# Releasing and casting batch 1's v on ScalarE, and cutting the key-value products of batches 4 to 7 into thirds

## The chip, the cores and the metric

The kernel runs on one core of one Trainium2 chip. The core has TensorE (PE: products, and loads of the stationary operand, PEld), VectorE (DVE), ScalarE (ACT), GpSimd (POOL) and SyncE (SP, which only issues transfers here). Each engine works through its own list of instructions in order; semaphores tie the lists together. The metric is the time of one execution on the device in microseconds. Before the change the median of three runs is 283.88 us (283.86 to 284.46).

## The reference

Eight batches of eight heads, 576 rows of 64 numbers each. Softmax of q goes over the 64 numbers of a row, softmax of k over the 576 rows; the small matrix kv of each head is multiplied onto q. Then comes a two-layer block over all 4,608 rows.

```python
q_s = softmax(q, axis=-1)               # (8, 8, 576, 64)
k_s = softmax(k, axis=2)
kv = np.einsum('bhsd,bhse->bhde', k_s, v)
x = np.einsum('bhsd,bhde->bhse', q_s, kv)
x = x.transpose(0, 2, 1, 3).reshape(8 * 576, 512)
h = x @ w_in                            # (4608, 2048)
out = np.maximum(0.01 * h, h) @ w_out   # (4608, 512)
```

## The kernel before

The two-layer block is cut into nine tiles of 512 rows. Layer 1 (L506) of a tile is 64 products of 512 columns into PSUM tiles `ph`; ScalarE applies the leaky function (L515) and leaves `gj`. Layer 2 (L527) is 64 products of 512 columns into `pout`; a copy (L521) and two stores follow for each 128 rows. Tile 0 differs: its layer 1 is done in two halves of 256 columns, in which `end_act` applies the function to pairs of columns groups j, j+1, and its layer 2 takes the four row groups in turn for each j. So each j of layer 2 needs one more column of `w_out_sb`, which arrives in eight pieces of two columns, issued by GpSimd.

The attention of batch b stands in between. Its inputs come by SP's queue (`load`). A core's partition holds 9 rows (R) of a head, and two halves of four heads each; H0 and H1 are slices of these. For k: the maximum over rows (`k_tree`, `k_allmax`), subtraction (`k_sub`), exponential (`k_exp`, ScalarE). For v: a cast to bf16 into `vb` (`v_cast`, once for each pair of heads gg = 0 and 1, so gg = 0 reads H0 and gg = 1 reads H1). The key-value products (`kv_quads`, L311) are 36 for each gg: for each of the 9 rows four products of 64x64 weights and 65 columns, one on each quarter of PE's array. The 65th column is a column of ones and gives the denominator. `kd_make` divides by it. The attention products (`cross`, L430) take `kd` as weights and the transposed q as columns; `attend` allocates two PSUM tiles and makes the four products of one or two gg. `x_keep` copies the result into `xT`, the input of layer 1.

The order of the work is written out by hand. `at(t, u, ...)` hangs functions on point u of tile t; for tile 0 the points 0 to 31 come after the leaky functions of the two halves (point 16 + j is column group j of the second half) and the points 32 to 47 after each j of layer 2. From tile 1 on, points 0 to 15 follow the column groups of layer 1 and points 16 to 31 follow every fourth product of layer 2. What a function emits goes to the end of each engine's list at that moment.

Three places matter.

- `more_loads` (L630), at point 20 of tile 0: it takes a buffer for batch 1's v, has GpSimd write one element of it from `kmax` (L632), and then issues v's two halves on SP. Because the transfers overwrite that element, they wait for the write, and the write waits for the maximum of batch 1's k. Behind them in SP's queue stands `hold_sync(1, ...)`, a small transfer that waits for w_out columns 10 and 11, and then the loads of batch 2.
- Points 20 and 32 of tile 0: GpSimd casts v's gg = 1 at the end of its list for batch 1, behind two subtractions for q and one for k; ScalarE casts gg = 0 and then does the exponential of k's half H0. At point 43 `kv(1)` makes 36 products of gg = 0, then 36 of gg = 1.
- `attend_kv(b)` (L457), at one point of each of the tiles 2 to 5, for b = 3 to 6: the long attention products of batch b (rows 0 to 7 of R: two fours of 512 columns), eight short ones for the last row, then the 72 key-value products of batch b+1. The short products and the key-value sums share two PSUM tiles `pokv`. PSUM tiles of one tag rotate through six buffers.

Of the kernel before, what the change touches and what calls it, by code (L numbers as in the profile page):

```python
# [20 lines left out]
R = 9  # L21
# [4 lines left out]
def kernel(  # L26
# [9 lines left out]
    nc = tc.nc  # L36
# [3 lines left out]
    B, H, S, D = q.shape  # L40
# [31 lines left out]
    def raw(name):  # L72
        return raw_pool.tile([P, HL, R, D], FP32, name=name, tag="raw")
# [13 lines left out]
    ALLH, ALLR = slice(0, HL), slice(0, R)  # L87
    RA, RB = slice(0, 4), slice(4, R)
    R1, R2, R3 = slice(4, 6), slice(6, 8), slice(8, R)
    st = [{} for _ in range(B)]  # L90
# [11 lines left out]
    identf = const_pool.tile([P, P], FP32)  # L102
# [29 lines left out]
    def k_begin(b):  # L132
        st[b]["ke"] = ke_pool.tile([P, R, HL, D], BF16, name="ke")
        st[b]["kmax"] = mx_pool.tile([P, HL, D], FP32, name="kmax")
        st[b]["kmaxT"] = mx_pool.tile([P, HL * D], FP32, name="kmaxT")
        st[b]["kall"] = mx_pool.tile([P, HL, D], FP32, name="kall")

    def k_tree(b, hs, steps=slice(0, 4)):
        n = hs.stop - hs.start
        ks = st[b]["k"][:, hs]  # L140
        if steps.start == 0:
            st[b]["t4"] = mx_pool.tile([P, HL, 4, D], FP32, name="t4")[:, 0:n]
        t4 = st[b]["t4"]
        t2, t1 = t4[:, :, 0:2], t4[:, :, 0]
        for o, i0, i1 in (
            (t4, ks[:, :, 0:4], ks[:, :, 4:8]),
            (t2, t2, t4[:, :, 2:4]),
            (t1, t1, t4[:, :, 1]),
            (st[b]["kmax"][:, hs], t1, ks[:, :, 8]),
        )[steps]:  # L150
            nc.vector.tensor_tensor(out=o, in0=i0, in1=i1, op=ALU.max)  # L151
# [29 lines left out]
    def k_sub(eng, b, hs):  # L181
        ks = st[b]["k"][:, hs]
        n = hs.stop - hs.start
        eng.tensor_tensor(  # L184
            out=ks,
            in0=ks,
            in1=st[b]["kall"][:, hs].unsqueeze(2).to_broadcast([P, n, R, D]),
            op=ALU.subtract,
        )

    def k_exp(b, hs):
        nc.scalar.activation(  # L192
            out=st[b]["ke"][:, :, hs].rearrange("p r h d -> p h r d"),
            in_=st[b]["k"][:, hs],
            func=AF.Exp,
        )

    def v_cast(eng, b, gg):
        o = vb2[b % 2][:, :, gg, :, 0:D].rearrange("p r h d -> p h r d")
        i = st[b]["v"][:, 2 * gg : 2 * gg + 2]  # L200
        if eng is nc.scalar:
            eng.copy(out=o, in_=i)
        else:
            eng.tensor_copy(out=o, in_=i)  # L204


    def q_begin(b):
        st[b]["qe"] = qe_pool.tile([P, R, HL, D], BF16, name="qe")
        if b < 2:
            st[b]["qT"] = qT_pool.tile([P, NB, R, L], BF16, name="qT", tag="qT")  # L210
# [70 lines left out]
    def q_exp(b, rs, hs=ALLH):  # L281
        nc.scalar.activation(  # L282
            out=st[b]["qe"][:, rs, hs].rearrange("p r h d -> p h r d"),
            in_=st[b]["q"][:, hs, rs],
            func=AF.Exp,
        )
# [16 lines left out]
        )  # L303


    def kv_quads(b, gg, outs):
        for r in range(R):
            for hp in range(2):
                for hh in range(2):
                    rows = slice(hh * L, (hh + 1) * L)  # L310
                    nc.tensor.matmul(  # L311
                        outs[hh][hp * D : (hp + 1) * D, 0 : D + 1],
                        lhsT=st[b]["ke"][rows, r, 2 * gg + hp],
                        rhs=vb2[b % 2][rows, r, gg, hp, 0 : D + 1],
                        start=(r == 0),
                        stop=(r == R - 1),
                    )

    def kv(b):

        pkv = [psB_pool.tile([P, 2, D + 2], FP32, name="pkv", tag=BANK_TAG) for _ in range(2)]
        for gg in range(2):
            kv_quads(b, gg, [pkv[hh][:, gg] for hh in range(2)])
        st[b]["pkv"] = pkv

    def kd_make(b):
        for hh in range(2):
            pkv = st[b]["pkv"][hh]
            krec = small_pool.tile([P, 2, 1], FP32, name="krec")
            nc.vector.reciprocal(out=krec, in_=pkv[:, :, D : D + 1])  # L330
            nc.vector.tensor_tensor(
                out=kd2[b % 2][:, :, hh],
                in0=pkv[:, :, 0:D],
                in1=krec.to_broadcast([P, 2, D]),
                op=ALU.mult,
            )
# [101 lines left out]
    def attend(b, ggs, rows):  # L438
        n = (rows.stop - rows.start) * L
        ps = [  # L440
            psB_pool.tile([P, len(ggs), n], FP32, name="po", tag=BANK_TAG) for _ in range(2)
        ]
        for i, gg in enumerate(ggs):
            cross(b, gg, [ps[hp][:, i] for hp in range(2)], rows)
        st[b]["po", ggs, rows.start] = ps

    def x_keep(eng, b, ggs, rows, hp):
        ps = st[b]["po", ggs, rows.start][hp]
        c0, c1 = b * S + rows.start * L, b * S + rows.stop * L
        s0 = 2 * ggs[0] + hp  # L450
        o = xT[:, s0 : 2 * ggs[-1] + hp + 1 : 2, c0:c1]
        if eng is nc.scalar:
            eng.copy(out=o, in_=ps)  # L453
        else:
            eng.tensor_copy(out=o, in_=ps)

    def attend_kv(b, rows=slice(0, 8), rest=slice(8, R)):  # L457
        keep = attend_rows(b, rows)
        n = 2 * (rest.stop - rest.start) * L
        both = [psB_pool.tile([P, n + 2 * (D + 2)], FP32, name="pokv", tag=BANK_TAG) for _ in range(2)]  # L460
        ps = [a[:, 0:n].rearrange("p (g c) -> p g c", g=2) for a in both]
        st[b + 1]["pkv"] = pkv = [a[:, n:].rearrange("p (g d) -> p g d", g=2) for a in both]
        for gg in range(2):
            cross(b, gg, [ps[hp][:, gg] for hp in range(2)], rest)
        for gg in range(2):
            kv_quads(b + 1, gg, [pkv[hh][:, gg] for hh in range(2)])
        st[b]["po", (0, 1), rest.start] = ps
        kd_make(b + 1)
        for fn in keep:
            fn()  # L470
        for hp in range(2):
            x_keep(nc.scalar, b, (0, 1), rest, hp)

    def attend_rows(b, rows, engs=(nc.scalar, nc.scalar)):
        groups = ((0, 1),) if rows.stop - rows.start <= 4 else ((0,), (1,))
        for ggs in groups:
            attend(b, ggs, rows)
        return [
            lambda ggs=ggs, hp=hp: x_keep(engs[hp], b, ggs, rows, hp) for ggs in groups for hp in range(2)
        ]  # L480
# [57 lines left out]
    def at(t, u, *fns):  # L538
        while t > 0 and u >= 32:
            t, u = t + 1, u - 32  # L540
        hooks.setdefault((t, u), []).extend(fns)
# [5 lines left out]
    H0, H1 = slice(0, 2), slice(2, 4)  # L547
# [9 lines left out]
    def hold_sync(i, src):  # L557
        nc.sync.dma_start(out=held[:, i], in_=src)
# [70 lines left out]

    def more_loads():  # L630
        st[1]["v"] = t = raw("v_raw")
        nc.gpsimd.tensor_copy(out=t[0:1, 0, 0, 0:1], in_=st[1]["kmax"][0:1, 1, D - 1 : D])  # L632
        load(v, 1, "v_raw", [(H0, ALLR), (H1, ALLR)], t)
        hold_sync(1, w_out_sb[0:1, 11, 0:128])
        st[2]["k"] = load(k, 2, "k_raw", [(H0, ALLR)])
        load(q, 1, "q_raw", [(ALLH, RE)], st[1]["q"])
        load(k, 2, "k_raw", [(H1, ALLR)], st[2]["k"])
        st[2]["q"] = load(q, 2, "q_raw", [(ALLH, ALLR)])
        st[2]["v"] = load(v, 2, "v_raw", [(ALLH, ALLR)])


    at(0, 19, lambda: q_max(0, R3), lambda: q_sub(nc.vector, 0, R3), lambda: q_exp(0, R3))
    at(0, 20, lambda: k_begin(1), lambda: q_begin(1), lambda: k_tree(1, H0), more_loads, lambda: k_tree(1, H1))
    at(0, 20, lambda: q_max(1, R7, H0), lambda: q_sub(nc.gpsimd, 1, R7, H0), lambda: k_allmax(1))
    at(0, 20, lambda: q_max(1, R7, H1), lambda: q_sub(nc.gpsimd, 1, R7, H1), lambda: k_sub(nc.vector, 1, H1))
    at(0, 20, lambda: k_sub(nc.gpsimd, 1, H0), lambda: v_cast(nc.gpsimd, 1, 1))
    at(0, 31, lambda: q_exp(1, R7, H0), lambda: q_sum(1, R7, H0), lambda: q_norm(1, R7, H0))
    at(0, 31, lambda: k_exp(1, H1))
    at(0, 32, lambda: q_exp(1, R7, H1), lambda: q_sum(1, R7, H1), lambda: q_norm(1, R7, H1))
    at(0, 32, lambda: q_sum(0, R3), lambda: q_norm(0, R3))  # L650
    at(0, 32, lambda: v_cast(nc.scalar, 1, 0), lambda: k_exp(1, H0))
    at(0, 42, lambda: q_turn_first(1, 0, R7), lambda: q_keep_first(nc.scalar, 1, 0, R7))
    at(0, 43, lambda: kv(1), lambda: kd_make(1))
    at(0, 44, lambda: q_turn_first(1, 1, R7), lambda: q_keep_first(nc.scalar, 1, 1, R7))
    at(0, 44, lambda: q_transpose(0, 8, 1), lambda: q_keep(nc.scalar, 0, 8, 1))
    at(0, 45, lambda: k_begin(2), lambda: q_begin(2), lambda: k_tree(2, H0))
# [53 lines left out]
    for t in range(3, B - 1):  # L710
        b = t + 1
# [140 lines left out]
```

## Time and profile before

| | us |
|---|---|
| median of three runs | 283.88 |
| the profiled execution | 284.06 |
| its span on the core | 282.3 |
| PE busy with products | 275.1 |
| ScalarE busy | 160.7 |
| VectorE busy | 159.7 |
| GpSimd busy | 55.4 |
| products of layer 1 (L506), 640 | 126.8 |
| products of layer 2 (L527), 592 | 128.2 |
| key-value products (L311), 576, outside and inside `attend_kv` | 3.8 + 3.4 |
| casts of v on GpSimd (L204), 14 | 25.6 |

A busy time of an engine is the time covered by its instructions; a product of 512 columns is shown with some 0.38 us, but products overlap, and in a dense stretch one starts every 0.216 us. So the starts say more than the durations. In a timeline, a row gives start, length, engine, line, operation and tiles, how many instructions are merged in it, and in brackets the idle time before it and what ended it. In the chain of work a row gives start, length and what was done. Times are from the span's start.

### The profile page before, as it was taken

How to read it: one execution, taken by the hardware profiler on the slowest of the kernel's cores; microseconds unless marked ns; L12 is line 12 of the kernel's file. 1: busy time of each engine (PE TensorE's matmuls, PEld its weight loads, DVE VectorE, ACT ScalarE, POOL GpSimd, SP SyncE). 2: the span in 40 equal slices, each digit the busy share in tenths (PEclk: the TensorE clock that was granted, in tenths of full speed). 3: DMA queues.
4: the chain of work that ended last, by engine and by line, in shares of the span. 5: the costliest groups of instructions: out<-in, count | busy, mean ns of one | idle time of the engine just before them, and what ended most of it. 6: DMA issues, size and time to landing. Idle time of an engine off the chain costs nothing.

```text
span 282.3 us, 5012 instructions
## 1 busy us (share of the span) xinstructions
PE 275.1 (97%) x2022; PEld 133.3 (47%) x2022; DVE 159.7 (57%) x225; ACT 160.7 (57%) x284; POOL 55.4 (20%) x54
## 2 busy tenths in 40 slices
PE   8899999999999999999999999999999999999994
PEld 2377645444444554445444544444444444444443
DVE  2975897999999939965885497634610000000021
ACT  4986564784489276755487448643844364146400
POOL 2847391358013005000500060000000000000000
PEclk9999999999999999999999999999999999999999
DMA  7999999996791597089409940332033200330033
GB/s 238 338 210 322 264 205 378 308 356 201 238 390 53 110 392 237 1 214 394 130 0 245 392 102 0 84 77 62 16 84 74 63 14 0 73 78 0 0 74 77
DMA packets 37207, 45.81 MB, mean 162 GB/s; under 512 B 16064, under 2 KB 20416, under 8 KB 37184
## 3 DMA queue, kind: packets, MB, share of 16 engines
q1 hardware_dynamic: 33696, 41.16, 45.9%
q0 software_dynamic: 3328, 4.20, 8.4%
q8 instruction: 16, 0.26, 0.4%
q10 hardware_dynamic: 160, 0.13, 0.1%
q14 instruction: 7, 0.06, 0.1%
HBM read 36.70 MB, written 9.44 MB: 163 GB/s over the span
## 4 chain that ended last, share of the span: by engine, by line
PE 83%; DMA 8%; POOL 4%; DVE 1%; SPq 1%; issue 0%; DVEq 0%
PE pout L527 41%; PE ph L506 39%; DMA q_raw<-in_q_dram 4%; DMA w_in_sb<-in_moe_w_in_dram 2%; DMA k_raw<-in_k_dram 2%; PE po L430 2%; POOL k_raw L184 1%; POOL vb L204 1%; POOL q_raw L274 1%; PE pokv L311 1%; DVE qmax L215 1%; POOL w_in_sb L124 1%; SPq L81 1%; PE pkv L311 1%; POOL qe L243 0%
## 5 line engine op out<-in xcount | busy, mean ns | idle before, releaser
L527 PE MATMUL pout<-w_out_sb,gj 128*128 128x512 bf16 (+2 forms) x592 | 128.2, 373 | 0.1
L506 PE MATMUL ph<-xT,w_in_sb 128*128 128x512 bf16 (+1 forms) x640 | 126.8, 358 | 0.2 <-DMA w_in_sb<-in_moe_w_in_dram 0.2
L515 ACT ACTIVATE gj<-ph 128x512 bf16<-128x512 f32 x144 | 82.3, 600 | 26.7 <-PE ph L506 26.4
L506 PEld LDWEIGHTS <-w_in_sb 128*128 128x128 bf16 x640 | 62.3, 98 | 62.5 <-DMA w_in_sb<-in_moe_w_in_dram 0.5
L527 PEld LDWEIGHTS <-gj 128*128 128x128 bf16 x592 | 56.4, 98 | 65.0 <-issue 0.6
L521 ACT COPY out_sb<-pout 128x512 f32<-128x512 f32 (+1 forms) x29 | 16.8, 579 | 66.2 <-PE pout L527 40.9
L521 DVE COPY out_sb<-pout 128x512 f32<-128x512 f32 (+1 forms) x8 | 4.8, 636 | 70.8 <-PE pout L527 70.8
L204 POOL CAST vb<-v_raw 128x1152 bf16<-128x1152 f32 x14 | 25.6, 1853 | 82.2 <-DMA v_raw<-in_v_dram 68.2
L291 DVE TENSOR_REDUCE qsum<-qe 128x36 f32<-128x2304 bf16 (+5 forms) x13 | 20.0, 1541 | 10.8 <-ACT qe L282 10.7
L192 ACT ACTIVATE ke<-k_raw 128x2304 bf16<-128x2304 f32 (+2 forms) x11 | 17.6, 1596 | 11.0 <-DVE k_raw L184 9.6
L298 DVE TENSOR_TENSOR qe<-qe,qrec 128x2304 bf16<-128x2304 bf16 (+5 forms) x13 | 22.7, 1746 | 0.4
L215 DVE TENSOR_REDUCE qmax<-q_raw 128x36 f32<-128x2304 f32 (+5 forms) x13 | 20.0, 1536 | 0.8 <-DMA q_raw<-in_q_dram 0.8
L282 ACT ACTIVATE qe<-q_raw 128x2304 bf16<-128x2304 f32 (+5 forms) x13 | 17.1, 1316 | 2.3 <-POOL q_raw L274 2.3
L184 DVE TENSOR_TENSOR k_raw<-k_raw,kall 128x2304 f32<-128x2304 f32 (+1 forms) x8 | 17.2, 2164 | 0.4
L453 ACT CAST xT<-po 128x512 bf16<-128x512 f32 (+3 forms) x35 | 15.7, 539 | 1.6 <-PE po L430 1.6
L274 POOL TENSOR_TENSOR q_raw<-q_raw,qmax 128x512 f32<-128x512 f32 (+3 forms) x7 | 12.2, 1738 | 19.8 <-DVE qmax L215 16.4
L151 DVE TENSOR_TENSOR t<-t 128x256 f32<-128x256 f32 (+2 forms) x22 | 14.7, 669 | 0.7
L151 DVE TENSOR_TENSOR t<-k_raw 128x512 f32<-128x512 f32 (+1 forms) x11 | 13.1, 1188 | 2.8 <-DMA k_raw<-in_k_dram 2.5
L330 DVE RECIPROCAL krec<-pokv 128x2 f32<-128x2 f32 x8 | 1.3, 164 | 22.2 <-PE pokv L311 22.2
L274 DVE TENSOR_TENSOR q_raw<-q_raw,qmax 128x2304 f32<-128x2304 f32 (+1 forms) x6 | 13.2, 2202 | 0.3
L342 PE MATMUL pout<-zero 128*128 128x512 bf16 x24 | 8.6, 500 | 1.3 <-POOL zero L99 1.3
L229 ACT ACTIVATE qe<-q_raw,nmax 128x64 bf16<-128x64 f32 x16 | 5.3, 333 | 3.4 <-DVE nmax L224 3.4
(65 smaller groups left out, 105.4 us busy)
## 6 DMA issues: line engine op xcount, KB each, us to landing
out_dram<-out_sb SPq DMA_DIRECT2D x70, 128.0 KB, 2.9
q_raw<-in_q_dram SPq DMA_DIRECT2D x6, 1152.0 KB, 8.6
v_raw<-in_v_dram SPq DMA_DIRECT2D x6, 1152.0 KB, 11.2
k_raw<-in_k_dram SPq DMA_DIRECT2D x5, 1152.0 KB, 6.2
k_raw<-in_k_dram SPq DMA_DIRECT2D x6, 576.0 KB, 5.9
v_raw<-in_v_dram SPq DMA_DIRECT2D x4, 576.0 KB, 7.8
w_in_sb<-in_moe_w_in_dram POOLq DMA_DIRECT2D x8, 256.0 KB, 7.3
w_out_sb<-in_moe_w_out_dram POOLq DMA_DIRECT2D x8, 256.0 KB, 12.8
```

What stands on the lines that cost most here:

```text
L151: nc.vector.tensor_tensor(out=o, in0=i0, in1=i1, op=ALU.max)
L184: eng.tensor_tensor(out=ks, in0=ks, in1=st[b]["kall"][:, hs].unsqueeze(2).to_broadcast([P, n, R, D]), op=ALU.subtract,)
L192: nc.scalar.activation(out=st[b]["ke"][:, :, hs].rearrange("p r h d -> p h r d"), in_=st[b]["k"][:, hs], func=AF.Exp,)
L204: eng.tensor_copy(out=o, in_=i)
L215: nc.vector.tensor_reduce(out=o, in_=st[b]["q"][:, hs, rs], axis=AX.X, op=ALU.max)
L274: eng.tensor_tensor(out=qs, in0=qs, in1=st[b]["qmax", rs.start, hs.start].unsqueeze(3).to_broadcast([P, m, n, D]), op=ALU.subtract,)
L291: nc.vector.reduce_sum(out=qsum, in_=st[b]["qe"][:, rs, hs], axis=AX.X)
L298: nc.vector.tensor_tensor(out=qes, in0=qes, in1=st[b]["qrec", rs.start, hs.start].unsqueeze(3).to_broadcast([P, n, m, D]), op=ALU.mult,)
L506: nc.tensor.matmul(ph, lhsT=w_in_sb[:, cb, j * P : (j + 1) * P], rhs=xT[:, cb, c0 : c0 + n], start=(cb == 0 and first), stop=(cb == NB - 1 ...
L515: nc.scalar.activation(out=o, in_=ph, func=AF.Prelu, alpha=LEAKY_SLOPE)
L521: copy(out=out_sb, in_=pout)
L527: nc.tensor.matmul(pout, lhsT=g_sb[j // 2][:, j % 2, tsub * P : (tsub + 1) * P], rhs=w_out_sb[:, j, os], start=(j == 0), stop=(j == NF - 1),)
```

## The change

Batch 1's v: its buffer is now written by ScalarE (one element, from the constant `identf`) at point 25 of tile 0 instead of by GpSimd at point 20, and all of `more_loads` moves there. Both casts of batch 1's v are on ScalarE, one after the other, ahead of the exponential of k's half H0. `kv(1)` makes the products of gg = 1 first.

`attend_kv`: the shared PSUM tiles are allocated first. The 72 key-value products are cut in three runs of 24 (rows 0 to 5 of gg = 0; rows 6 to 8 of gg = 0 and 0 to 2 of gg = 1; rows 3 to 8 of gg = 1), with the four long attention products of gg = 0 behind the first run, those of gg = 1 behind the second, and the eight short ones behind the third. The copies keep their order.

```diff
-    def kv_quads(b, gg, outs):
-        for r in range(R):
+    def kv_quads(b, gg, outs, rs=ALLR):
+        for r in range(R)[rs]:
...
-    def kv(b):
+    def kv(b, order=(0, 1)):
...
-        for gg in range(2):
+        for gg in order:
             kv_quads(b, gg, [pkv[hh][:, gg] for hh in range(2)])
...
     def attend_kv(b, rows=slice(0, 8), rest=slice(8, R)):
-        keep = attend_rows(b, rows)
         n = 2 * (rest.stop - rest.start) * L
...
+        part = lambda gg, r0, r1: kv_quads(b + 1, gg, [pkv[hh][:, gg] for hh in range(2)], slice(r0, r1))
+        part(0, 0, 6)
+        attend(b, (0,), rows)
+        part(0, 6, R)
+        part(1, 0, 3)
+        attend(b, (1,), rows)
+        part(1, 3, R)
         for gg in range(2):
             cross(b, gg, [ps[hp][:, gg] for hp in range(2)], rest)
-        for gg in range(2):
-            kv_quads(b + 1, gg, [pkv[hh][:, gg] for hh in range(2)])
+        keep = [lambda gg=gg, hp=hp: x_keep(nc.scalar, b, (gg,), rows, hp) for gg in range(2) for hp in range(2)]
...
     def more_loads():
         st[1]["v"] = t = raw("v_raw")
-        nc.gpsimd.tensor_copy(out=t[0:1, 0, 0, 0:1], in_=st[1]["kmax"][0:1, 1, D - 1 : D])
+        nc.scalar.copy(out=t[0:1, 0, 0, 0:1], in_=identf[0:1, 0:1])
...
-    at(0, 20, lambda: k_begin(1), lambda: q_begin(1), lambda: k_tree(1, H0), more_loads, lambda: k_tree(1, H1))
+    at(0, 20, lambda: k_begin(1), lambda: q_begin(1), lambda: k_tree(1, H0), lambda: k_tree(1, H1))
...
-    at(0, 20, lambda: k_sub(nc.gpsimd, 1, H0), lambda: v_cast(nc.gpsimd, 1, 1))
+    at(0, 20, lambda: k_sub(nc.gpsimd, 1, H0))
+    at(0, 25, more_loads)
...
-    at(0, 32, lambda: v_cast(nc.scalar, 1, 0), lambda: k_exp(1, H0))
+    at(0, 32, lambda: v_cast(nc.scalar, 1, 0), lambda: v_cast(nc.scalar, 1, 1), lambda: k_exp(1, H0))
...
-    at(0, 43, lambda: kv(1), lambda: kd_make(1))
+    at(0, 43, lambda: kv(1, (1, 0)), lambda: kd_make(1))
```

## The prediction

> **What bounds the kernel now.** First the page: busy times and the chain that ended last.
>
> ```profile
> span 282.3 us, 5012 instructions
> PE 275.1 (97%) x2022; PEld 133.3 (47%) x2022; DVE 159.7 (57%) x225; ACT 160.7 (57%) x284; POOL 55.4 (20%) x54
> ...
> PE 83%; DMA 8%; POOL 4%; DVE 1%; SPq 1%; issue 0%; DVEq 0%
> ```
>
> TensorE (PE) sets the end; the granted clock is 9 tenths or more in every slice, so the clock leaves nothing. A change counts only as far as it closes a gap in PE's stream or makes PE's own work shorter, and the small shares of DMA and POOL on the chain show where PE depended on others. Second, the chain in order of time and PE's timeline, in the stretch before the last place where POOL stands in it:
>
> ```profile
> 34.96 2.74 POOL q_raw L274
> 37.70 3.43 POOL k_raw L184
> 41.13 1.97 POOL vb L204
> 43.10 0.04 issue
> 43.14 0.48 PE pkv L311 x36
> ```
>
> ```profile
> 38.57 0.59 PE L527 MATMUL pout<-w_out_sb,gj 128*128 128x512 bf16 x2
> ...
> 42.51 0.48 PE L311 MATMUL pkv<-vb,ke 64*64 64x65 bf16 x36
> 43.14 0.48 PE L311 MATMUL pkv<-vb,ke 64*64 64x65 bf16 x36 [0.15 <-POOL vb L204]
> 43.55 0.82 PE L527 MATMUL pout<-w_out_sb,gj 128*128 128x512 bf16 x3
> ```
>
> The reader sees two holes. Batch 1's second 36 key-value products wait for POOL's cast (L204, done 43.09). And a layer-2 product starts at 38.57 although the one before started at 38.04 (start in the timeline of single products); neighbours stand 0.216 us apart, so 0.31 us are lost. That product opens the fifth pair of w_out columns, whose load ends just then: the issues of 24.7 to 25.4 us land at most 13.8 us later, so the one at 24.7 at 38.5. After 48 us no product of PE waits for another engine (the waits of PE from 48 us on are empty). Third, one stage that holds the attention of batch 3 and the key-value products of batch 4, and the last of these four stages:
>
> ```profile
> 102.87 0.63 PE L430 MATMUL po<-qX,kd 64*64 64x512 bf16 x8
> 103.33 0.23 PE L430 MATMUL pokv<-qX,kd 64*64 64x64 bf16 x8
> 103.39 0.87 PE L311 MATMUL pokv<-vb,ke 64*64 64x65 bf16 x72
> 104.19 0.61 PE L527 MATMUL pout<-w_out_sb,gj 128*128 128x512 bf16 x2
> ```
>
> ```profile
> 186.53 0.63 PE L430 MATMUL po<-qX,kd 64*64 64x512 bf16 x8
> ...
> 187.79 0.39 PE L527 MATMUL pout<-w_out_sb,gj 128*128 128x512 bf16 x1
> ```
>
> From first attention product to next layer-2 product: 1.32, 1.32, 1.29 and 1.27 us (starts 102.87, 128.46, 157.51, 186.53). Products here go in fours, one for each 64x64 quarter of the array. In the single starts the first five or six fours of key-value products stand 0.032 us apart, the products inside a four 3.3 ns; from then on they come singly, 8.3 ns apart, with pauses of 15 to 35 ns. PE's instructions then arrive slower than they could run: a load and a product each 8.3 ns, 4.1 ns an instruction. In batch 2's run straight behind layer 2 (69.00) ten fours go by before that starts.
>
> **The change part by part.**
>
> *Batch 1's cast.* Removed: POOL's cast (2.02 us at 41.07) and its one-element write L632. Added: a second ScalarE cast and a one-element ScalarE copy. The cast costs what its twin costs, 1.14 us. ScalarE's first cast ends at 39.73 and its k_exp starts only at 41.16, since it waits for POOL's k_sub (end 41.13); so the new cast runs 39.7 to 40.9 in an idle hole, if v's second half has landed. That half was issued at 29.3 and landed 10.0 us later (v loads of this stretch: 7.7 and 10.0), at 39.3. The order of halves is swapped: the half that needs k_exp at 37.35 and the new cast goes first at 42.51; the other, needing k_exp's end at 42.32, follows at 42.51 + 0.053 + 8 x 0.032 = 42.82. The hole closes: 43.14 - 42.82 = **-0.32 us**. Behind the cast on ScalarE stand k_exp and batch 1's copy of transposed q; the next user after them is the attention at 46.75, with 1.9 us of ScalarE idle in between. POOL's next work is at 51.59, so freeing it gives nothing.
>
> *The release of v.* The ScalarE copy stands behind the fifth of the eight second-half activations, 28.93 + 0.60 = 29.53; the copy itself I take at 0.21 us (ScalarE's 128x1 activation of L105, its nearest row), in gaps of 0.28 us, so PE does not see it. v's two loads leave SP at about 29.8 instead of 28.84, 0.9 us later; SP's next entry waits for w_out until 39.95 anyway, so nothing behind them moves. v's second half lands between 39.3 (if it was held back by the q loads ahead, not by its issue) and 40.2. At 40.2 the cast ends at 41.35, k_exp at 42.5, still before 42.82. The price if the cover goes: beyond a landing of 40.5 each us costs PE a us. Meanwhile w_out has the DMA engines longer for itself: 0 to -0.31 us for the hole at 38.57. Of the 16 landing events of that piece fourteen lie between 34.5 and 36.4 and only two at 38.0 and 38.5, and these two parts also ended the q loads last (32.5 and 33.1, long after v's issue); on them v would start behind q in either case. So I stay near the lower end: **-0.1 us**.
> The Trainium skill (DMA: Bandwidth & Descriptors, Queues, rings and completion order) says that each DMA engine shares its time in turn between the queues that have work. By that rule 0.9 us without v's queue is full gain for w_out, the whole 0.31, and the total below would be 0.2 larger; the two late parts speak for less.
>
> *Thirds.* No product is added or taken away; 24 key-value products, four long ones, 24, four, 24, then the eight short ones. Before each run of 24 (48 instructions) stands a long four of 0.216 us or layer 2, in which at 4.1 ns some 50 instructions arrive. So every run should go at 0.032. One stage: first six fours 0.053 + 5 x 0.032 = 0.213; long 0.216; six fours 0.19; long 0.216; 0.19; eight short 0.03 and 0.135 to the next layer-2 product (216.01 to 216.15, the stage of batch 7). Sum 1.19. Against 1.32 + 1.32 + 1.29 + 1.27 = 5.20: 5.20 - 4.76 = **-0.44 us**. Bounds: +0.67 (each switch priced, below) and -0.45. The keys' k_exp ends 1.2 us or more before the stages (127.26 for 128.46 at the closest), casts and transposed q earlier, so the earlier start meets nothing late. The order of PSUM tiles changes: the tiles of the rest and the key-value sums are now the next layer-1 tile's first; ScalarE leaves them at 105.9, layer 1 starts at 107.81. With that cover gone, each us would be PE's.
>
> Sum: -0.32 - 0.1 - 0.44 = -0.86. The profiled run took 284.06 us in all for its span of 282.3, so 283.2; it lies 0.18 above the median of the runs (283.88), which gives **283.0 us**.
>
> **The rivals.**
>
> *A. v comes late, slower.* The casts now stand in order on ScalarE ahead of k_exp. If v's second half needs 11.7 us from issue, as the whole v loads from 60 us on do, it lands at 30.2 + 11.7 = 41.9; cast until 43.05, k_exp until 44.2, second half of products at 44.27 instead of 43.14: +1.13. With thirds at -0.44: +0.7, **284.6**. It decides from a landing near 41.3, where the loss eats the thirds. For it: the loads' times scatter from 7.7 to 11.7 here. Against: the stretch from 38.5 on has a DMA share of 0.85 and falling, v was nearly through.
>
> *B. The thirds bring nothing.* If the 8.3 ns pace is not cured by a long four ahead, the stages stay at 5.20: -0.42, **283.5**. For it: the last stage has the same order and loses less (1.27), so something besides the order matters; DMA share is 0.05 there, 1.04 in the others. Against: the run at 69.00.
>
> *C. Each switch costs.* PE enters 64x64 work from layer 2 with 0.09 us on top (42.20 to 42.51 instead of 0.216). If key-value to attention and back cost that too, the three additional switches in four stages cost 12 x 0.093 = 1.12; -0.45 + 1.12 = +0.67, with -0.42: +0.25, **284.1**. Against: attention to short attention to key-value goes at 0.206 and 0.03, without a surcharge.
>
> **How the numbers follow.** Forecast 0.62, A 0.12, B 0.18, C 0.08. About 0.2% (0.57 us) is what a measurement of this kernel tells from no change. The forecast with its bounds (282.7 to 283.4) is mostly beyond that: 0.55 faster; B and the forecast's upper edge and half of C give 0.31 within; A and half of C, with what they may hide, 0.14 slower. The range runs from 282.6 (w_out's full gain) to 284.2, leaving most of A out.
>
> **What would show it.** Right: no POOL cast between 41 and 43, second half of batch 1's products right behind the first, and stages of 1.17 to 1.22 us with fours 0.03 apart. v's loads issued near 29.8; the hole at 38.57 shows who was right on w_out. Wrong: k_exp of batch 1 starting after 41.5 with v's landing as its releaser (A); stages still 1.27 to 1.32 (B) or longer, with gaps where the kinds meet (C).

## The result and the profile after

Seven runs of each, taken beside each other: 283.02 us (282.68 to 283.38) against 284.10 us (283.80 to 284.46). The ratio is 0.9964, 95% interval 0.9952 to 0.9976, so 0.7 to 1.4 us faster, 1.0 in the middle. The profiled execution took 282.68 us with a span of 280.9.

From the page of the changed kernel, the span and the shares of the chain of work by engine; behind them the waits of PE from 20 us on (in total, times, longest):

```profile
span 280.9 us, 5008 instructions
...
PE 92%; DVE 3%; DMA 2%; ACT 1%; issue 0%; SPq 0%
```

```profile
PE psum_qt L403 <- DVE qe L298: 0.3, 1, 0.3
```

GpSimd has left the chain, and the only wait that PE has left from 20 us on lies ahead of everything that was changed. The stretch of batch 1, in PE's timeline and in ScalarE's (start, length, engine, line, operation, idle before and its releaser):

```profile
41.24 0.59 PE L532 MATMUL pout<-w_out_sb,gj 128*128 128x512 bf16 x2
41.77 0.78 PE L311 MATMUL pkv<-vb,ke 64*64 64x65 bf16 x72
42.48 0.82 PE L532 MATMUL pout<-w_out_sb,gj 128*128 128x512 bf16 x3
```

```profile
38.28 1.14 ACT L202 CAST vb<-v_raw 128x1152 bf16<-128x1152 f32 x1
39.70 1.15 ACT L202 CAST vb<-v_raw 128x1152 bf16<-128x1152 f32 x1 [0.28 <-DMA v_raw<-in_v_dram]
40.86 1.16 ACT L192 ACTIVATE ke<-k_raw 128x1152 bf16<-128x1152 f32 x1
```

The 72 products are now one row: 0.72 us from the first to the next layer-2 product, where it had been 1.04. ScalarE's second cast waits 0.28 us for v's second half, and k_exp then starts without a pause and ends at 42.02. Its products start at 42.07: the first 36 are nine fours, and in the single starts the tenth four stands there, 0.05 behind the end of k_exp. Where products did wait for k_exp, in the experiments below, they also started 0.05 behind it. So nothing is left of the cover here. Nor could k_exp have begun much sooner: GpSimd's subtraction for the keys, which it needs too, ended at 40.82, 0.04 before the cast.

The layer-2 products around the fifth pair of w_out columns now follow each other without a break (six products in 1.46 us, where the kernel before had two, a hole, and the next at 38.57):

```profile
37.83 1.46 PE L532 MATMUL pout<-w_out_sb,gj 128*128 128x512 bf16 x6
```

One stage of the attention of batch 3 and the key-value products of batch 4:

```profile
101.80 0.38 PE L311 MATMUL pokv<-vb,ke 64*64 64x65 bf16 x24
102.02 0.39 PE L430 MATMUL po<-qX,kd 64*64 64x512 bf16 x4
102.23 0.36 PE L311 MATMUL pokv<-vb,ke 64*64 64x65 bf16 x24
102.42 0.39 PE L430 MATMUL po<-qX,kd 64*64 64x512 bf16 x4
102.64 0.36 PE L311 MATMUL pokv<-vb,ke 64*64 64x65 bf16 x24
102.83 0.26 PE L430 MATMUL pokv<-qX,kd 64*64 64x64 bf16 x8
103.02 0.39 PE L532 MATMUL pout<-w_out_sb,gj 128*128 128x512 bf16 x1
```

All four stages take 1.22 us. From the single starts they are 4.875 us together, against 5.187: -0.31. The hole in front of the fifth pair of w_out columns is gone (0.31). So the two profiles differ in the changed places by 0.33 + 0.31 + 0.31 = 0.95 us. The spans differ by 1.38; the rest of 0.43 lies ahead of the first thing changed (layer 2 begins at 30.92 instead of 31.35, most of it a hole of 0.36 at 23.48 that of the two only the profile before has), and the experiments show that this part scatters from execution to execution.

### The profile page after: what moved, and what is told of

Its sections match the earlier page's. It is cut to its first block, busy times and chain, and to the rows that moved or that the text cites. A ratio compares the mean times of both kernels' runs of the same rounds, so it can differ in the third digit from the quotient of the medians.

```text
span 280.9 us, 5008 instructions
## 1 busy us (share of the span) xinstructions
PE 274.5 (98%) x2022; PEld 133.1 (47%) x2022; DVE 159.3 (57%) x225; ACT 161.8 (58%) x286; POOL 53.4 (19%) x52
## 4 chain that ended last, share of the span: by engine, by line
PE 92%; DVE 3%; DMA 2%; ACT 1%; issue 0%; SPq 0%
PE pout L532 45%; PE ph L511 43%; DMA k_raw<-in_k_dram 2%; PE po L430 2%; DVE t L151 1%; PE pokv L311 1%; PE pkv L311 1%; DVE qe L298 0%; DVE qsum L291 0%; DVE k_raw L380 0%; ACT vb L202 0%; PE psum_q L254 0%; ACT ke L192 0%; PE psum_qt L403 0%; ACT qe L282 0%
## 5 line engine op out<-in xcount | busy, mean ns | idle before, releaser
L526 ACT COPY out_sb<-pout 128x512 f32<-128x512 f32 (+1 forms) x29 | 16.8, 579 | 66.0 <-PE pout L532 43.8
L204 POOL CAST vb<-v_raw 128x1152 bf16<-128x1152 f32 x13 | 24.4, 1901 | 81.2 <-DMA v_raw<-in_v_dram 58.2
L274 DVE TENSOR_TENSOR q_raw<-q_raw,qmax 128x2304 f32<-128x2304 f32 (+1 forms) x6 | 13.2, 2203 | 0.6 <-issue 0.5
L311 PEld LDWEIGHTS <-ke 64*64 64x64 bf16 x576 | 6.7, 107 | 4.2 <-issue 2.5
```

The lines of the kernel that those rows point to most:

```text
L274: eng.tensor_tensor(out=qs, in0=qs, in1=st[b]["qmax", rs.start, hs.start].unsqueeze(3).to_broadcast([P, m, n, D]), op=ALU.subtract,)
L526: copy(out=out_sb, in_=pout)
```

## The experiments

Each ratio is against the kernel before on the same chip, with its 95% interval.

**The thirds alone**: `attend_kv` of the changed kernel in the kernel before.

```diff
+        part(0, 0, 6)
+        attend(b, (0,), rows)
+        part(0, 6, R)
+        part(1, 0, 3)
+        attend(b, (1,), rows)
+        part(1, 3, R)
```

> Only attend_kv is changed (thirds); batch 1's v is released and cast as before. My theory (each part of the change pays by itself): the four stages take 1.22 us each instead of 1.32, 1.32, 1.29, 1.27, so -0.31 us; the two holes, at the second half of batch 1's key-value products (0.33 us over a dense stream) and at the fifth pair of w_out columns (0.31), stay. Time about 0.3 us below the kernel before, ratio 0.999. Rival (most of the 1.08 us comes from the stages, since PE is also less disturbed behind them): 0.8 us or more below.

Measured: 283.49 us against 283.86, ratio 0.9987 (0.9978 to 0.9996). Stages 1.22 to 1.23 us, and the first hole stays:

```profile
42.02 0.48 PE L311 MATMUL pkv<-vb,ke 64*64 64x65 bf16 x36
42.66 0.48 PE L311 MATMUL pkv<-vb,ke 64*64 64x65 bf16 x36 [0.16 <-POOL vb L204]
```

The hole at w_out is there too, but only 0.13 us. The theory holds; the thirds do not carry the whole gain.

**The release alone.**

```diff
-        nc.gpsimd.tensor_copy(out=t[0:1, 0, 0, 0:1], in_=st[1]["kmax"][0:1, 1, D - 1 : D])
+        nc.scalar.copy(out=t[0:1, 0, 0, 0:1], in_=identf[0:1, 0:1])
...
-    at(0, 20, lambda: k_sub(nc.gpsimd, 1, H0), lambda: v_cast(nc.gpsimd, 1, 1))
+    at(0, 20, lambda: k_sub(nc.gpsimd, 1, H0))
+    at(0, 25, more_loads, lambda: v_cast(nc.gpsimd, 1, 1))
```

> Only the release of batch 1's v is moved (ScalarE write at point 25); GpSimd still casts gg = 1, the order of the halves and attend_kv are as before. Theory: v's loads are issued some 0.9 us later, the fifth piece of w_out lands before layer 2 needs it, the hole of 0.31 us at that product is gone, while the wait for GpSimd's cast stays: about 0.3 us below the kernel before. Rival (that landing scatters from execution to execution and the release has nothing to do with it): the hole is there or not as in the kernel before, time the same within 0.1 us.

Measured: 283.71 us against 283.86, ratio 0.9995 (0.9986 to 1.0004): half of what was expected, and not told from nothing. The hole at w_out is gone. But see PE's timeline behind it:

```profile
42.39 0.48 PE L311 MATMUL pkv<-vb,ke 64*64 64x65 bf16 x36 [0.33 <-ACT ke L192]
43.15 0.48 PE L311 MATMUL pkv<-vb,ke 64*64 64x65 bf16 x36 [0.28 <-POOL vb L204]
43.56 0.39 PE L527 MATMUL pout<-w_out_sb,gj 128*128 128x512 bf16 x1
```

PE is earlier at batch 1's products, and waits: first for k_exp, which in the old order is needed at once, then for GpSimd's cast, which still ends at 43.10. It leaves for layer 2 at 43.56, where the kernel before left at 43.55. What the closed hole gave, and the 0.20 us by which layer 2 had begun earlier (31.15 against 31.35), is given back at the next waits.

**The casts alone**: both on ScalarE and gg = 1 first, with the early release by GpSimd.

```diff
-    at(0, 20, lambda: k_sub(nc.gpsimd, 1, H0), lambda: v_cast(nc.gpsimd, 1, 1))
+    at(0, 20, lambda: k_sub(nc.gpsimd, 1, H0))
...
-    at(0, 32, lambda: v_cast(nc.scalar, 1, 0), lambda: k_exp(1, H0))
+    at(0, 32, lambda: v_cast(nc.scalar, 1, 0), lambda: v_cast(nc.scalar, 1, 1), lambda: k_exp(1, H0))
...
-    at(0, 43, lambda: kv(1), lambda: kd_make(1))
+    at(0, 43, lambda: kv(1, (1, 0)), lambda: kd_make(1))
```

> Only the casts are changed: both of batch 1's v on ScalarE, gg = 1 first in the products; the release stays with GpSimd at point 20, attend_kv as before. Theory: the wait for the cast goes (-0.33 us), the hole at the fifth pair of w_out columns stays (0.31 us, product at 0.53 us from the one before). About 0.3 us below the kernel before. Rival (the hole at w_out depends on the execution): it may be gone here too, then 0.6 us below in that execution.

Measured: medians 283.58 against 283.86; two runs, at 284.77 and 285.05, make the ratio uncertain, 0.9996 (0.9983 to 1.0008). The trace is clear: the stage takes 0.71 us without a wait, and the hole at w_out is there with 0.25 us.

**The kernel before once more.**

> The kernel before once more, for a second profile. If the hole at the fifth pair of w_out columns belongs to the early release of v, it is there again with 0.2 to 0.4 us; if it scatters, it can be gone. The hole of 0.36 us at 23.48 us (a product of layer 1 that waits for the last piece of w_in), which nothing in the change touches and which the changed kernel's profile did not have, should be of another size here.

One run, 284.34 us. The hole at w_out was gone here, so its size does scatter: the fifth piece landed at 38.06 and PE needed it at 38.19; 0.05 us were lost at the next piece instead. But PE, earlier for it, then waited at batch 1 on both halves, as k_exp and GpSimd's cast were 0.26 us later than in the first profile:

```profile
42.63 0.48 PE L311 MATMUL pkv<-vb,ke 64*64 64x65 bf16 x36 [0.39 <-ACT ke L192]
43.40 0.48 PE L311 MATMUL pkv<-vb,ke 64*64 64x65 bf16 x36 [0.29 <-POOL vb L204]
```

In the starts, 0.46 us were lost ahead of the first half and 0.46 between the halves, where the first profile lost 0.33 in all. So what is not lost at w_out can be lost at batch 1, without any change to the kernel.

The hole at 23.5 was 0.28 us. Five of the profiles taken, of various kernels, have this one (0.28, 0.28, 0.36, 0.36 and 0.53 us); six others wait for w_in near 20 us instead, 0.55 to 0.82 us, and two do neither; layer 2 began anywhere from 30.92 to 31.63. The profile of the changed kernel has the earliest start of all, and these are the 0.43 us by which it was lucky.

What the release does to the fifth piece is seen better in its time from issue to landing (the largest of the issues between 24 and 25 us). Released by GpSimd at point 20: 13.8, 13.2, 13.6, 13.7 us in four profiles. By ScalarE at point 25: 12.4 to 13.0 us in eight. At point 29, below: 10.6. The groups do not touch. Here the kernel before, the changed kernel, and the one with the release at point 29 (issues of w_out pieces: duration in ns, first and last start; below them the least, middle and longest time from issue to landing):

```profile
L129 POOL DMA_DIRECT2D w_out_sb<-in_moe_w_out_dram x2: 733/737/741, 24.0 to 24.7; - x2
...
DMA to landing us min/median/max: 11.7/12.8/13.8
```

```profile
L129 POOL DMA_DIRECT2D w_out_sb<-in_moe_w_out_dram x2: 721/727/733, 23.8 to 24.5; - x2
...
DMA to landing us min/median/max: 10.5/11.6/12.7
```

```profile
L129 POOL DMA_DIRECT2D w_out_sb<-in_moe_w_out_dram x2: 723/728/733, 24.1 to 24.9; - x2
...
DMA to landing us min/median/max: 10.0/10.3/10.6
```

The queues show why. The one microsecond from 33 to 34, in the kernel before and with the release at point 29 (q0 is GpSimd's queue with w_out, q1 SP's with v; packets, MB, share of the 16 engines):

```profile
q1 hardware_dynamic: 86, 0.20, 57.0%
q0 software_dynamic: 92, 0.09, 55.2%
```

```profile
q0 software_dynamic: 215, 0.20, 123.9%
```

Beside v, w_out gets 0.09 MB in a microsecond; without it, 0.20. In all thirteen profiles v's packets begin in numbers 3.5 to 3.7 us after v's first half is issued, and in the microsecond before that SP's queue moves at most 0.03 MB. v's second half lands 9.8 to 10.3 us after its own issue, whatever the release. So v's transfer goes where its issue goes.

**Release and casts without the thirds**: the changed kernel with the old `attend_kv`.

```diff
+        keep = attend_rows(b, rows)
...
-        part(0, 0, 6)
...
+        for gg in range(2):
+            kv_quads(b + 1, gg, [pkv[hh][:, gg] for hh in range(2)])
```

> The changed kernel with attend_kv as before: release and casts of batch 1's v without the thirds. Theory (release and casts pay only together: the release alone brings PE earlier to a wait for GpSimd's cast that stands where it stood): 0.5 to 0.65 us below the kernel before, more than the 0.15 and 0.28 that the two gave alone, stages as before at 1.32, 1.32, 1.29, 1.27. Rival (they only add up): 0.4 below.

Measured: 283.34 us against 283.87, ratio 0.9978 (0.9968 to 0.9988), so 0.53 us by the medians. The stage of batch 1 takes 0.71 us, and there is no hole at the fifth pair:

```profile
42.05 0.78 PE L311 MATMUL pkv<-vb,ke 64*64 64x65 bf16 x72
```

The two parts gave 0.15 and 0.28 alone; together they give more, though the intervals of the single parts are too wide to exclude a plain sum. The traces show why they belong together: the release closes a hole ahead of the wait that the casts remove.

**The old order of batch 1's halves.**

```diff
-    at(0, 43, lambda: kv(1, (1, 0)), lambda: kd_make(1))
+    at(0, 43, lambda: kv(1), lambda: kd_make(1))
```

> The changed kernel, but batch 1's products in the old order, gg = 0 first. Theory: gg = 0 needs the end of k_exp of half H0, which comes about 0.3 us after PE arrives at this stage (42.02 against 41.77 in the changed kernel's profile), so the first 36 products wait about 0.3 us and the time is 0.3 us above the changed kernel, 0.6 to 0.7 below the kernel before. Rival (the swap is idle, the ScalarE cast alone closes the hole): same as the changed kernel, the stage still 0.72 us long.

Measured: 283.39 us against 284.04, ratio 0.9972 (0.9960 to 0.9984). That is 0.65 us below the kernel before, where it was expected, but the interval overlaps those of the changed kernel (0.9964 and, below, 0.9966), so the times do not settle it. PE's and ScalarE's timelines:

```profile
41.17 1.03 PE L532 MATMUL pout<-w_out_sb,gj 128*128 128x512 bf16 x4
42.24 0.80 PE L311 MATMUL pkv<-vb,ke 64*64 64x65 bf16 x72
```

```profile
41.03 1.16 ACT L192 ACTIVATE ke<-k_raw 128x1152 bf16<-128x1152 f32 x1
```

The stage itself is 0.74 us long, but the wait stands ahead of it: the first product starts 0.425 us behind the last layer-2 product instead of 0.309 as in the changed kernel, and 0.05 behind the end of k_exp (42.19). So the old order waits for k_exp as the theory says, 0.12 us in this profile instead of 0.3: layer 2 had begun 0.36 us later than in the changed kernel's profile, and k_exp ended only 0.17 later. What the swap is worth hangs on how early PE is in an execution.

**A later release**, for the price of a late v.

```diff
-    at(0, 25, more_loads)
+    at(0, 29, more_loads)
```

> The changed kernel, with v released two activations later (point 29 of tile 0). Theory (the price of a late v, rival A of the prediction): v is issued 1.74 us later, its second half lands near 41.4 instead of 39.7, the second cast ends at 42.6 and k_exp at 43.7; the second 36 products start near 43.8 instead of 42.1, time 1.6 us above the changed kernel and 0.5 above the kernel before. Rival (on the parts of the transfer that end last v follows q whatever its issue): v lands before 40.5 and the time is as in the changed kernel within 0.3 us.

Measured: 284.17 us against 284.04, ratio 1.0002 (0.9993 to 1.0011). The gain of the changed kernel is gone. ScalarE's and PE's timelines:

```profile
41.65 1.15 ACT L202 CAST vb<-v_raw 128x1152 bf16<-128x1152 f32 x1 [1.70 <-DMA v_raw<-in_v_dram]
42.70 1.16 ACT L192 ACTIVATE ke<-k_raw 128x1152 bf16<-128x1152 f32 x1
```

```profile
42.85 0.48 PE L311 MATMUL pkv<-vb,ke 64*64 64x65 bf16 x36 [0.51 <-ACT vb L202]
43.92 0.48 PE L311 MATMUL pkv<-vb,ke 64*64 64x65 bf16 x36 [0.59 <-ACT ke L192]
```

v's second half lands at 41.62, the cast waits 1.7 us for it, and k_exp stands behind the cast. The expected chain is there. That the second half starts at 43.9, near the expected 43.8, is in part chance, since PE was itself half a us late here (the hole at 23.5 is 0.53 us). In the starts the two waits lose 1.34 us. That is less than the expected 1.6, as v's second half landed 9.76 us after its issue instead of 10.06. The runs say 1.1 us over the changed kernel's ratio.

**No cut: all key-value products first.**

```diff
-        part(0, 0, 6)
-        attend(b, (0,), rows)
-        part(0, 6, R)
-        part(1, 0, 3)
-        attend(b, (1,), rows)
-        part(1, 3, R)
+        part(0, 0, R)
+        part(1, 0, R)
+        attend(b, (0,), rows)
+        attend(b, (1,), rows)
```

> The changed kernel, with all 72 key-value products ahead of the attention products in attend_kv (no cut). Theory (PE's instructions run out): as at batch 2, some 40 products go by at 0.032 us a four before they come singly; the 18 fours take 0.63 us instead of 0.59, a stage 1.25 to 1.27 us, together 0.1 to 0.2 us above the changed kernel, about 0.2 below the old order. Rival (the cut itself is what counts): the stages are back at 1.27 to 1.32.

Measured: 283.00 us against 284.04, ratio 0.9957 (0.9942 to 0.9972). Stages 1.297, 1.233, 1.208 and 1.207 us, 4.945 together. The third:

```profile
156.45 0.78 PE L311 MATMUL pokv<-vb,ke 64*64 64x65 bf16 x72
157.04 0.62 PE L430 MATMUL po<-qX,kd 64*64 64x512 bf16 x8
...
157.66 0.39 PE L530 MATMUL pout<-w_out_sb,gj 128*128 128x512 bf16 x1
```

Of the 0.31 us that the thirds save, 0.24 come from the order alone, the key-value products directly behind layer 2, without any cut. That is more than the theory gave it, and the four runs do not tell this kernel from the changed one. In two of the stages the uncut run is even faster than the thirds. In the first stage it is slower by 0.08: there one more wait instruction stands in PE's list (at 102.484, 51 ns), and the attention product starts 0.085 us behind the last key-value product instead of 0.01 to 0.03. That this instruction is the cause was not tried by itself.

**Two runs of 36.**

```diff
+        part(0, 0, R)
+        attend(b, (0,), rows)
+        part(1, 0, R)
+        attend(b, (1,), rows)
```

> The changed kernel, with the key-value products in two runs of 36 (gg = 0, long attention of gg = 0, gg = 1, long attention of gg = 1, short ones) instead of three of 24. Theory (PE's instructions run out): 36 products are 72 instructions, and while they run at 0.032 us a four some 70 more arrive; neither run should fall to single products, so stages of 1.22 us as with thirds, or 1.19 if the short products at the end are then not starved. Rival (a run has to fit in what PE holds when it begins, 48 instructions do and 72 don't): the end of each run goes at 8.3 ns a product with pauses, stages of 1.25 to 1.29 us.

Measured: 283.22 us against 284.04, ratio 0.9968 (0.9951 to 0.9984); stages 1.309, 1.246, 1.245, 1.246 us. The rival is nearer. The first run of 36, behind layer 2, goes through at full pace. The second, behind a long four, does so for 32 products and then comes singly: in the second stage the starts stand 0.030 us apart by fours up to 128.98, then 129.014, .023, .031, .039, .048, and the long attention products behind them come singly too.

This profile shows one thing more, at batch 1, where the kernel is the changed one. v had landed in time (40.23), but k_exp waited for GpSimd's subtraction, and the second half of the products lost 0.13 us:

```profile
41.69 1.16 ACT L192 ACTIVATE ke<-k_raw 128x1152 bf16<-128x1152 f32 x1 [0.29 <-POOL k_raw L184]
```

So GpSimd can still come back into the chain.

**The changed kernel again, and the short products first.** The second kernel moves the eight short attention products ahead of the first run.

```diff
+        for gg in range(2):
+            cross(b, gg, [ps[hp][:, gg] for hp in range(2)], rest)
         part(0, 0, 6)
...
         part(1, 3, R)
-        for gg in range(2):
-            cross(b, gg, [ps[hp][:, gg] for hp in range(2)], rest)
```

> The changed kernel once more, on the chip of the next two. 0.8 to 1.1 us below the kernel before; stages of 1.22 us; v's second half lands between 39.4 and 40.3 and ScalarE's second cast starts behind it, no hole at the fifth pair of w_out columns.

> The changed kernel with the eight short attention products ahead of the first run of 24 instead of behind the third. Theory (after a long four some 64 instructions of PE go at full pace and then they come singly: so far 8 to 9 fours after an attention product, 13 to 17 behind layer 2): now 48 instructions stand behind each long four, none is starved, and the way out to layer 2 takes 0.13 us instead of 0.16: stages of 1.18 to 1.19 us, 0.12 to 0.15 us below the changed kernel. Rival (the way out costs the same whatever stands last): stages of 1.22 us, time the same.

Measured on one chip, against 283.87: the changed kernel 282.97 us, ratio 0.9966 (0.9954 to 0.9979), stages of 1.22; the other one 282.80 us, ratio 0.9958 (0.9946 to 0.9971). Its second-last stage:

```profile
156.49 0.26 PE L430 MATMUL pokv<-qX,kd 64*64 64x64 bf16 x8
156.57 0.36 PE L311 MATMUL pokv<-vb,ke 64*64 64x65 bf16 x24
156.76 0.39 PE L430 MATMUL po<-qX,kd 64*64 64x512 bf16 x4
156.98 0.36 PE L311 MATMUL pokv<-vb,ke 64*64 64x65 bf16 x24
157.17 0.39 PE L430 MATMUL po<-qX,kd 64*64 64x512 bf16 x4
157.39 0.36 PE L311 MATMUL pokv<-vb,ke 64*64 64x65 bf16 x24
157.68 0.39 PE L532 MATMUL pout<-w_out_sb,gj 128*128 128x512 bf16 x1
```

All four stages take 1.19 us, 0.03 less each, as expected; no product comes singly any more. The times agree with 0.12 us less, but the intervals overlap, so the stages show it and the runs alone do not. In the changed kernel's second profile v's second half landed at 39.85, as expected, and there is no hole at the fifth pair. Both profiles lose a little at the sixth pair instead, 0.09 and 0.05 us: the next piece of w_out is now the one that only just arrives.

## Why the prediction held, step by step

**The cast** was predicted at -0.32 us and measured at -0.33 (stage of 1.04 to 0.72 us). The idle hole on ScalarE was where the prediction put it, the landing came at 39.7, inside its 39.3 to 40.2, and the cast alone removed the wait. That the size fits to 0.01 is in part luck: the second profile of the kernel before lost 0.91 us at this place, with PE earlier. In the profiles that have release, casts and swap the cover is between nothing and 0.15 us, and in one 0.13 was missing.

**The release** was the mis-sized term: -0.1 us predicted, -0.31 between the two profiles. The failed step is the argument from the two late parts of the transfer, "on them v would start behind q in either case". SP's queue lay almost empty before v's packets came, and v began 3.5 to 3.7 us after its issue at every release. On average v was issued 0.87 us later against the fifth piece in the eight profiles with the release at point 25 than in the four with the early one, and that piece landed 0.9 us sooner after its issue; at point 29 it landed another 2 us sooner. The Trainium skill's rule (DMA: Bandwidth & Descriptors, Queues, rings and completion order), by which an engine shares its time in turn between the queues that have work, was worked out in the prediction to the full 0.31. By that rule w_out has to lose while v moves, and the trace agrees: 0.09 MB in a microsecond beside v, 0.20 without it.

How much this is worth in an execution depends on when layer 2 begins: with the early release the four profiles lost 0.31, 0.05, 0.13 and 0.25 us at the fifth or sixth pair, 0.19 in the mean, so the 0.31 is the top of what was seen. And it shows in the time only as far as the cast is out of the way, which the prediction added up without saying.

**The thirds** were predicted at -0.44 and gave -0.31 (stages of 1.22 instead of 1.19). The three runs and the two long fours took what was said; the way out did not. It was taken at 0.135 us from a stage that ends in short products behind long ones; here the short ones follow 48 instructions of the third run, the last of them come singly (102.859, .866, .870, .904), and the way out is 0.16. Moving them to the front gave the 1.19, 4.759 us for the four stages, the prediction's 4.76.

**The sum** is -0.95 in the changed places of the two profiles against -0.86 predicted; the runs say -1.08 and, in the second comparison, -0.90. Two terms were off, by 0.2 in one direction and 0.13 in the other, and nearly cancelled. The kernel before had a median of 284.10 beside the changed one, where the forecast started from 283.88; this adds 0.2 to the measured difference. So the hit on 283.0 (measured 283.02) is in part luck, while the signs and the places of all three terms are not.

**The rivals.** A, a late v: not in the changed kernel, but its mechanism is real, as the release at point 29 shows, and so is the price that the prediction put on it. Its limit of 40.5 was 2.0 us ahead of PE's arrival at 42.51. With the late release PE would have arrived at 42.27, v landed 1.35 us past that limit, and 1.34 were lost. B, the pace is not cured: wrong, since runs of 24 behind a long four go through at full pace. But the cut is not what most of the gain needs: 0.24 of the 0.31 come already with all 72 directly behind layer 2. C, a price for each switch: wrong; three more switches in a stage, and 0.19 us for each six fours as without them.

## What to carry to other kernels

When two waits stand one behind the other on the engine that sets the end, closing the first alone moves the time into the second: close both, and test them together. When a transfer is held back on purpose, its release has a window. Of the three release points tried here only the middle one spared both the weights ahead of it and the cast behind it, with nothing to 0.15 us to spare in most profiles; point 29, 1.74 us later, already cost the whole gain. In this kernel the key-value products went best in runs of 24, each behind layer 2 or a long four, with the short attention products ahead of them all.

## What the hardware showed that was not expected

Products on 64x64 quarters go in fours at 0.030 to 0.033 us only for a while. Behind a long four of 0.216 us this held for 56 to 66 instructions in three orders (the kernel before, thirds, halves; with the short ones first so many never came in a row), then the products came singly, 4.1 ns for an instruction, with pauses. The pauses are what costs: a four at full pace is eight instructions in 0.032 us, 4.0 ns each, hardly less than 4.1. From the twenty-first key-value product on, the kernel before took 9.7 ns for a product in the first of its four stages and 9.0 in the last, against 7.8 in a run of the thirds. Behind a long stretch of layer 2 the full pace held for 100 to 136 instructions, and in batch 1 of the changed kernel's profile for all 144. The Trainium skill (TensorE: Matmul & The Clock Gate, header table) gives TensorE a queue of 64 instructions; the 56 to 66 agree with that, the 100 to 144 do not follow from it. That PE's instructions run out is therefore argued from these counts and not shown, and why a long stretch lets more of them through was not tried.

The start of the kernel scatters by up to 0.7 us (layer 2 from 30.92 to 31.63) with the landing of pieces of w_in, in kernels that are the same up to there. A difference of two single profiles of this kernel is good to about half a us unless that part is taken out.
